# Head-pair preparation moved to the front of its slot, with the sequence mixing spaced by other products

## The chip, the cores and the metric

The kernel runs on one core of a Trainium2 chip. The metric is the device time of one execution in microseconds; a second number, the span, runs from the first to the last instruction that the profiler recorded. TensorE multiplies matrices and transposes (a product with an identity matrix), VectorE, ScalarE and GpSimd (POOL) do element-wise work, SyncE (SP) issues most of the loads and stores. ScalarE has a queue for loads of its own. Each engine runs its own instructions in the order in which they stand in its list and waits where an operand isn't there.

## The reference

Three layers, all in float32, with B = 2 sequences of S = 768 positions, 8 heads of 64, model width 512:

```
scores = q k^T / 8 - slope(head) * distance          # kept: 96 local positions and the first 8 (global)
a = softmax(scores);  x = a v                        # x: (2, 768, 512), heads side by side
u = x + (x^T U V)^T                                  # sequence mixing, U 768x32, V 32x768
x = u + relu(u w_ch1) w_ch2                          # 512 -> 2048 -> 512
xk, xr = mixes of x with x shifted by one position
out = sigmoid(xr w_r) * (relu(xk w_k)^2 w_v)         # 512 -> 1024 -> 512
```

The weights arrive as 64-bit floats and are turned into pairs of float32r numbers (high and low part) on the chip; each large product is three products of such parts.

## The kernel before

The body first runs attention in windows (`attention_windows`, lines 155 to 382), then the second layer, then the third. Work is written as lists of small steps; `weave` (line 594) merges several lists by the relative place of each step in its own list, so a list of two steps put beside one of sixteen has its steps after the fourth and the twelfth. The merged order is a priority: the framework's planner then fixes each engine's list, mostly in that order, but lets a later instruction go ahead where it thinks an earlier one isn't ready yet.

**Head pairs.** The 16 heads of both sequences make 8 pairs. For each pair, `load_qk` (line 170) loads Q and K, four loads of 192 KB on SP's queue, into one buffer for Q and one for K. `load_v` (line 182) loads V, twice, with a shifted copy, in six loads into two buffers. `qprep` (line 253) transposes Q by six TensorE instructions into two PSUM banks and copies them scaled to QS on ScalarE in two copies. `kprep` (line 266) does the same for K into KK, and GpSimd copies the first 32 columns to each block (line 282). `score(pp, i0)` (line 285) multiplies for two blocks of 128 positions and two heads; VectorE adds the mask and takes the minimum (line 301), ScalarE takes the exponential and its sum (line 304). `norm` (line 307) divides, on GpSimd (line 315). `trans` (line 321) transposes the result on TensorE, copied by VectorE or ScalarE (lines 472 and 474). `pv` (line 332) multiplies with V.

**Slots.** `slot(pp)` (line 348) lists the steps in which pair pp is scored, pair pp-1 is transposed and multiplied with V, and pair pp+1 is prepared: load of V; scores of blocks 0 and 1; transposes; `qprep` of the next pair; scores of blocks 2 and 3; normalisation; transposes; `kprep` of the next pair; loads of Q and K for the pair after the next; the rest. There are nine slots. The PSUM banks are in two groups of four: scores and first products of each layer use group "a", everything else group "t". The `in` pool has one buffer for each of Q and K, so the load of the next Q waits until the present Q is transposed.

**Side work.** Beside the slots, `side` (line 625) places other steps: constants in slot 1, `u_steps(0)` in slot 5, `st_split(0)` in slot 6, the first products of the second layer in slots 7 and 8. `CONV` spreads weight conversions (`bg`). `u_steps(b)` (line 498) is the sequence mixing of sequence b, 16 steps: six groups of transposes (`tr`), `gms` with 12 products with U, `gs` with six small copies and sums on ScalarE and VectorE in a chain, and eight products with V (`hm`, line 525), each added to `yp` by VectorE (line 530). `u_split` (line 546) splits one 512-column chunk of `yp` into high and low parts, a ScalarE copy and a VectorE subtraction (lines 551 and 552). `m_ch1` (line 567) and `m_ch2` (line 582) are the products of the second layer, 12 each. After the last slot come `u_steps(1)` woven with the first half of `st_ch2(0, 0)`, the other half woven with `st_split` of chunk 1 (lines 633 and 702), and from line 704 on a long run of products.

**The start.** Line 196 loads Q of pair 0 on SP, `limits` (line 49) loads the two numbers n_global and n_local on ScalarE's queue and turns them into floats on VectorE, `warm` runs products with zeros on TensorE, then K of pair 0 is loaded on SP. Lines 375 to 381 then prepare pair 0, with `windows` (line 214), the mask, in between, and load Q and K of pair 1 and V of pair 0.

Of the kernel before, what the change touches and what calls it, by code (L numbers as in the profile page):

```python
# [19 lines left out]
NT = S // 128  # L20
# [13 lines left out]
def body(tc, out, q, k, v, n_global, n_local, U, V, w1, w2, mu_k, mu_r, wk, wv, wr):  # L34
    nc = tc.nc
    with ExitStack() as ctx:
# [11 lines left out]

        def limits():
            nraw = const.tile([128, 2], I64, name="nraw")  # L50
            nfl = const.tile([128, 2], F32, name="nfl")
            nc.scalar.dma_start(out=nraw[:, 0:1], in_=n_global.rearrange("(o n) -> o n", o=1).partition_broadcast(128))
            nc.scalar.dma_start(out=nraw[:, 1:2], in_=n_local.rearrange("(o n) -> o n", o=1).partition_broadcast(128))
            nw = nraw.bitcast(I32).rearrange("p (n w) -> p n w", w=2)
            nlo = nraw.bitcast(U32).rearrange("p (n w) -> p n w", w=2)
            nc.vector.tensor_copy(out=nf, in_=nw[:, :, 1])
            nc.vector.tensor_copy(out=nfl, in_=nlo[:, :, 0])
            nc.vector.scalar_tensor_tensor(out=nf, in0=nf, scalar=4294967296.0, in1=nfl, op0=ALU.mult, op1=ALU.add)
# [96 lines left out]
        def attention_windows(pool, actx, cctx, bctx, bank, ecopy):  # L155
# [13 lines left out]

            def load_qk(pp, names="qk"):  # L170
                b, p = PRS[pp]
                z = st[pp]
                for nm in names:
                    src = q if nm == "q" else k
                    z[nm] = in_p.tile([128, NT, 2, D], F32, tag=nm + "in", name=nm + "in")
                    for t in range(2):
                        nc.sync.dma_start(out=z[nm][:, :, t, :],
                                          in_=src[b, 2 * p + t].rearrange("(t p) d -> p t d", p=128))
# [16 lines left out]

            load_qk(0, "q")
            limits()
            wz = ac.tile([128, 512], mybir.dt.bfloat16, name="wz")
            nc.vector.memset(wz, 0.0)
# [6 lines left out]

            warm(8)
            load_qk(0, "k")


# [3 lines left out]
            def windows():  # L214
# [12 lines left out]
                m1 = scratch(F32, 256, "m1")  # L227
                nc.vector.tensor_scalar(out=m0, in0=relf, scalar1=0.0, scalar2=None, op0=ALU.is_ge)
                nc.vector.tensor_scalar(out=m1, in0=relf, scalar1=nl, scalar2=None, op0=ALU.is_lt)
                nc.vector.tensor_tensor(out=m0, in0=m0, in1=m1, op=ALU.mult)  # L230
                nc.gpsimd.memset(DW, BIG)
                nc.vector.copy_predicated(W1[:, 0:96], m0[:, 32:128].bitcast(U32), relf[:, 32:128])
# [7 lines left out]
                nc.vector.tensor_copy(out=W0, in_=W1[:, 128:256])  # L240
                nc.vector.tensor_tensor(out=W0[:, 0:32], in0=W0[:, 0:32], in1=dg, op=ALU.min)


# [104 lines left out]
            def slot(pp):  # L348
                o = pp - 1
                cur, nxt, pre = pp < NPR, pp + 1 < NPR, pp >= 1  # L350
                s = []

                def add(cond, f, *a):
                    if cond:
                        s.append(lambda: f(*a))
                add(cur and pp, load_v, pp)
                add(cur, score, pp, 0)
                add(pre, trans, o, 0, 0)
                add(pre, trans, o, 1, 0)
                add(nxt, qprep, pp + 1)  # L360
                add(cur, score, pp, 2)
                add(cur, norm, pp, 0, 3)
                add(pre, trans, o, 0, 1)
                add(pre, trans, o, 1, 1)
                add(nxt, kprep, pp + 1)
                add(pp + 2 < NPR, load_qk, pp + 2)
                add(cur, score, pp, 4)
                add(cur, norm, pp, 3, 6)
                add(pre, trans, o, 0, 2)
                add(pre, trans, o, 1, 2)  # L370
                add(pre, pv, o, 0)
                add(pre, pv, o, 1)
                return s

            qprep(0)
            warm(3)
            windows()
            kprep(0)
            warm(3)
            load_qk(1)  # L380
            load_v(0)
            return {"zt_p": zt_p, "slot": slot, "constants": constants}

        def path(general):
            if general:
                attention_general()
            with ExitStack() as pctx:
# [110 lines left out]
                def u_steps(b):  # L498
# [38 lines left out]

                    steps += [gms, gs]
                    for c0, c1 in ((0, 512), (512, 768)) if b == 0 else ((0, 256), (256, 768)):
# [81 lines left out]
                else:  # L621
                    actx, bctx, cctx = ExitStack(), ExitStack(), ExitStack()
                    A = attention_windows(pool, actx, cctx, bctx, bank, ecopy)
                    xt_p[0] = A["zt_p"]
                    side = {1: lambda: [A["constants"]], 5: lambda: u_steps(0), 6: lambda: st_split(0, slot_a),
                            7: lambda: st_ch1(0, 0, slot_b)[:2], 8: lambda: st_ch1(0, 0, slot_b)[2:]}
# [5 lines left out]
                open_slots("sd")  # L632
                weave(u_steps(1), st_ch2(0, 0)[:2])
                actx.close()
# [64 lines left out]
                def st_mix(c, which, mk):  # L699
                    return [lambda kk=kk: m_mix(c, which, kk, mk) for kk in range(4)]  # L700

                weave(st_ch2(0, 0)[2:],
                      [lambda kk=kk: u_split(1, kk, slot_d) for kk in range(4)])
                weave(st_ch1(0, 1, slot_c), [lambda kk=kk: u_split(2, kk, slot_d) for kk in range(4)])
# [53 lines left out]
```

## Time and profile before

| what | value |
|---|---|
| runs shown | 572.84, 572.85, 568.08 us; median 572.84 |
| profiled execution | 567.52 us |
| its span | 565.7 us, 7722 instructions |
| TensorE busy (matmul) | 537.9 us, 95% of the span |
| VectorE, ScalarE, GpSimd busy | 324.4 us (57%), 230.4 us (41%), 182.9 us (32%) |
| mean granted TensorE clock | 0.985 of full speed |

Matmuls are pipelined and their ends are modelled, so a busy share of TensorE is no share of its peak. Busy times of stages, waits and the timeline are read from the same execution.

### The profile page before, as it was taken

To read this page: it belongs to the slowest core of one execution; us is meant where nothing else is said; L and a number is where in the kernel's file an instruction comes from. 1 tells how busy PE (TensorE), PEld (TensorE's weight loads), DVE (VectorE), ACT (ScalarE), POOL (GpSimd) and SP (SyncE) were. 2 spreads that over 40 slices of the span, in tenths; PEclk is the share of its full clock that TensorE was granted. 3 is DMA by queue.
4 is the path that set the end of the run, shared out by engine and by line. 5 is a ranking of instruction groups with operands and counts; after the bars stand their busy time and mean duration, and the time that the engine had idled before them with its cause. 6 is when DMAs were issued, how large, how long until landed. Compare 5 with 4: busy or idle time off the path is not lost.

```text
span 565.7 us, 7722 instructions
## 1 busy us (share of the span) xinstructions
PE 537.9 (95%) x2814; PEld 435.2 (77%) x2814; DVE 324.4 (57%) x703; ACT 230.4 (41%) x525; POOL 182.9 (32%) x223
## 2 busy tenths in 40 slices
PE   6898779899799999999999999999999999999996
PEld 3676657587588888888888888888788888888886
DVE  4657598998798726364282855579833442243101
ACT  3888678774445204032222242144361243124200
POOL 1555533770253104040120340254571244024200
PEclk9898899999899999999999999999999999999999
DMA  8865745444036402213040404004101000100011
GB/s 162 162 159 117 184 115 146 158 126 149 1 111 187 148 1 80 69 40 109 1 151 0 123 27 149 0 1 148 39 0 38 19 20 0 38 19 20 1 38 43
DMA packets 60206, 43.84 MB, mean 78 GB/s; under 512 B 51648, under 2 KB 51904, under 8 KB 60160
## 3 DMA queue, kind: packets, MB, share of 16 engines
q1 hardware_dynamic: 59872, 43.27, 27.2%
q8 instruction: 24, 0.39, 0.3%
q14 instruction: 22, 0.18, 0.1%
q10 hardware_dynamic: 288, 0.00, 0.0%
HBM read 40.11 MB, written 3.15 MB: 76 GB/s over the span
## 4 chain that ended last, share of the span: by engine, by line
PE 79%; DVE 8%; ACT 7%; POOL 2%; issue 2%; SPq 1%; DMA 1%; POOLq 0%; DVEq 0%; ACTq 0%
PE aps L575 23%; PE bps L588 20%; PE pvs L693 12%; PE kps L666 10%; PE prs L682 6%; ACT P L304 3%; PE s L294 2%; DVE cvc L423 2%; PE tp L329 2%; POOL P L315 2%; PE xb L342 1%; DVE cvc L425 1%; DVE P L301 1%; DMA qin<-in_q_dram 1%; PE hps L527 1%
## 5 line engine op out<-in xcount | busy, mean ns | idle before, releaser
L588 PE MATMUL bps<-rs,w2s 128*128 128x512 f32 x576 | 134.5, 393 | 0.5 <-DVE xt L474 0.3
L575 PE MATMUL aps<-us,w1s 128*128 128x512 f32 x576 | 133.9, 390 | 0.0
L588 PEld LDWEIGHTS bps<-rs,w2s 128*128 128x128 f32 x576 | 109.1, 190 | 23.7 <-DVE xt L474 0.5
L575 PEld LDWEIGHTS aps<-us,w1s 128*128 128x128 f32 x576 | 107.8, 188 | 22.5 <-issue 0.2
L578 ACT ACTIVATE rs<-aps 128x512 fp32r<-128x512 f32 x48 | 28.2, 593 | 102.8 <-PE aps L575 102.8
L666 PE MATMUL kps<-mix,wk 128*128 128x512 f32 x288 | 66.1, 389 | 1.2 <-DVE kf L671 1.2
L666 PEld LDWEIGHTS kps<-mix,wk 128*128 128x128 f32 x288 | 54.0, 188 | 12.8 <-DVE kf L671 1.6
L693 PE MATMUL pvs<-wv,kh 128*128 128x512 f32 (+1 forms) x208 | 61.8, 373 | 0.0
L579 DVE SCALAR_TENSOR_TENSOR rs<-aps,rs 128x512 fp32r<-128x512 f32 x48 | 32.8, 686 | 45.5 <-ACT rs L578 45.5
L315 POOL TENSOR_SCALAR P<-P,sm 128x256 f32<-128x256 f32 (+1 forms) x96 | 47.8, 518 | 28.9 <-DVE sm L311 10.6
L423 DVE SCALAR_TENSOR_TENSOR cvc<-cvc,cvt 128x512 uint32<-128x512 uint32 (+2 forms) x55 | 51.6, 940 | 9.7 <-ACT cvc L422 8.3
L422 ACT ACTIVATE cvc<-stg 128x512 f32<-128x512 f32 (+2 forms) x55 | 36.2, 665 | 44.9 <-DMA stg<-in_moe_w_ch_dram 18.2
L592 DVE TENSOR_TENSOR yp<-bps,yp 128x512 f32<-128x512 f32 (+1 forms) x64 | 33.9, 551 | 29.8 <-PE bps L588 29.8
L304 ACT ACTIVATE P<-P,nm 128x256 f32<-128x256 f32 (+1 forms) x96 | 46.2, 484 | 11.6 <-DVE nm L301 11.3
L432 POOL TENSOR_TENSOR w2s<-cvc,w2s 128x512 fp32r<-128x512 f32 x16 | 23.5, 1485 | 70.0 <-ACT w2s L430 70.0
L432 POOL TENSOR_TENSOR w1s<-cvc,w1s 128x512 fp32r<-128x512 f32 x16 | 23.6, 1492 | 69.2 <-ACT w1s L430 69.1
L648 POOL TENSOR_SCALAR mixt<-yp,mu 128x512 f32<-128x512 f32 (+1 forms) x32 | 21.6, 681 | 74.3 <-DVE mixf L650 29.8
L425 DVE SCALAR_TENSOR_TENSOR cvc<-stg,cvc 128x512 uint32<-128x512 uint32 (+1 forms) x54 | 44.8, 839 | 0.4
L693 PEld LDWEIGHTS pvs<-wv,kh 128*128 128x128 f32 x208 | 38.1, 188 | 6.9
L673 POOL TENSOR_TENSOR kl<-kf,kh 128x512 fp32r<-128x512 f32 x24 | 31.0, 1293 | 31.1 <-ACT kh L672 31.1
L301 DVE CUSTOM_DVE_ANT_0 P<-s,DW 128x256 f32<-128x256 f32 (+1 forms) x96 | 33.5, 395 | 10.8 <-PE s L294 10.7
L693 PE MATMUL pvs<-wv,kl 128*128 128x512 f32 (+1 forms) x104 | 38.8, 373 | 0.0
(104 smaller groups left out, 640.8 us busy)
## 6 DMA issues: line engine op xcount, KB each, us to landing
stg<-in_moe_w_ch_dram SPq DMA_DIRECT2D x32, 512.0 KB, 4.0
stg<-in_moe_w_k_dram SPq DMA_DIRECT2D x8, 512.0 KB, 3.7
stg<-in_moe_w_v_dram SPq DMA_DIRECT2D x8, 512.0 KB, 3.7
qin<-in_q_dram SPq DMA_DIRECT2D x16, 192.0 KB, 3.5
kin<-in_k_dram SPq DMA_DIRECT2D x16, 192.0 KB, 3.4
vin<-in_v_dram SPq DMA_DIRECT2D x16, 192.0 KB, 3.4
out_dram<-sg SPq DMA_DIRECT2D x11, 256.0 KB, 2.0
stg<-in_moe_w_r_dram SPq DMA_DIRECT2D x4, 512.0 KB, 3.8
```

Source lines behind the costliest of these rows:

```text
L301: nc.vector.tensor_tensor_reduce(out=P[:, t, 0:n], in0=sps[t][:, 256 * x:256 * x + n], in1=W, scale=2.0 ** -(2 * p + t + 1), scalar=TOP, o ...
L304: nc.scalar.activation(out=P[:, t, 0:n], in_=P[:, t, 0:n], func=ACTF.Exp, scale=-1.0, bias=z["nm"][:, i, t:t + 1], accum_out=z["sm"][:, i, ...
L315: nc.gpsimd.tensor_scalar(out=Pl, in0=Pl, scalar1=z["sm"][:, i, t:t + 1], scalar2=1.0, op0=ALU.mult, op1=ALU.mult)
L422: nc.scalar.activation(out=c.bitcast(F32), in_=Hh.bitcast(F32), func=ACTF.Copy, scale=2.0 ** -112)
L423: nc.vector.scalar_tensor_tensor(out=c, in0=c, scalar=3, in1=t, op0=ALU.logical_shift_left, op1=ALU.bitwise_or)
L425: nc.vector.scalar_tensor_tensor(out=c if plain is None else plain, in0=Hh, scalar=0x80000000, in1=c, op0=ALU.bitwise_and, op1=ALU.bitwise_or)
L432: nc.gpsimd.tensor_tensor(out=lo, in0=f, in1=hi.bitcast(F32), op=ALU.subtract)
L575: nc.tensor.matmul(ps, lhsT=wsl(("w1", g), lw, kk, f * 128, 128), rhs=us[c][:, lx, kk, :], start=(n == 0), stop=(n == 11))
L588: nc.tensor.matmul(ps, lhsT=wsl(("w2", g), lw, f, o * 128, 128), rhs=r[:, lx, f, :], start=(n == 0), stop=(n == 11))
L666: nc.tensor.matmul(ps, lhsT=wsl("wk", lw, kk, f * 128, 128), rhs=xk[:, lx, kk, :], start=(n == 0), stop=(n == 11))
L682: nc.tensor.matmul(pr, lhsT=xr[:, lx, kk, t * 128:(t + 1) * 128], rhs=wsl("wr", lw, kk, 0, 512), start=(n == 0), stop=(n == 11))
L693: nc.tensor.matmul(pv, lhsT=ks[c][lx][:, f, t * 128:(t + 1) * 128], rhs=wsl("wv", lw, f, c0, c1 - c0), start=(n == 0), stop=(n == 23))
```

## The change

In words:

- In `slot`, `qprep(pp+1)` stands ahead of the first scores of pair pp, and `kprep(pp+1)` and `load_qk(pp+2)` right behind them, ahead of the transposes of the pair before.
- Q has two buffers instead of one. K keeps one.
- K of pair 0 is loaded on ScalarE's queue, behind the two limits. The order at the start is: Q of pair 0 (SP), zeros and warm products, the part of the mask that needs no limits, the limits, K of pair 0 (ScalarE's queue), Q and K of pair 1 and V of pair 0 (SP), `qprep(0)`, the rest of the mask, `kprep(0)`. Before, the last three loads stood behind `kprep(0)`.
- Scratch for the zeros and the limits comes from the pool of the score tiles.
- Of `u_steps(0)`, the first eight steps (transposes, `gms`, `gs`) stay in slot 5 and the eight `hm` go to slot 6, ahead of the splits.
- Of the second sequence, the first eight steps of `u_steps(1)` are woven with one `m_ch2`; then three `m_ch2` follow alone, then the eight `hm`, then the splits of chunk 1 alone.

```diff
@@ load_qk
-            def load_qk(pp, names="qk"):
+            def load_qk(pp, names="qk", eng=nc.sync):
...
-                    z[nm] = in_p.tile([128, NT, 2, D], F32, tag=nm + "in", name=nm + "in")
+                    z[nm] = in_p.tile([128, NT, 2, D], F32, tag=nm + "in", name=nm + "in", bufs=2 if nm == "q" else 1)
                     for t in range(2):
-                        nc.sync.dma_start(out=z[nm][:, :, t, :],
+                        eng.dma_start(out=z[nm][:, :, t, :],
...
             load_qk(0, "q")
-            limits()
-            wz = ac.tile([128, 512], mybir.dt.bfloat16, name="wz")
+            wz = np_p.tile([128, 512], mybir.dt.bfloat16, tag="P", name="wz")
...
             warm(8)
-            load_qk(0, "k")
@@ windows: now a generator in two parts
                 nc.vector.tensor_scalar(out=m0, in0=relf, scalar1=0.0, scalar2=None, op0=ALU.is_ge)
+                nc.gpsimd.memset(DW, BIG)
+                yield
                 nc.vector.tensor_scalar(out=m1, in0=relf, scalar1=nl, scalar2=None, op0=ALU.is_lt)
                 nc.vector.tensor_tensor(out=m0, in0=m0, in1=m1, op=ALU.mult)
-                nc.gpsimd.memset(DW, BIG)
@@ slot
                 add(cur and pp, load_v, pp)
+                add(nxt, qprep, pp + 1)
                 add(cur, score, pp, 0)
+                add(nxt, kprep, pp + 1)
+                add(pp + 2 < NPR, load_qk, pp + 2)
                 add(pre, trans, o, 0, 0)
                 add(pre, trans, o, 1, 0)
-                add(nxt, qprep, pp + 1)
                 add(cur, score, pp, 2)
                 add(cur, norm, pp, 0, 3)
                 add(pre, trans, o, 0, 1)
                 add(pre, trans, o, 1, 1)
-                add(nxt, kprep, pp + 1)
-                add(pp + 2 < NPR, load_qk, pp + 2)
                 add(cur, score, pp, 4)
...
+            wins = windows()
+            next(wins)
+            limits(lambda dt, n, nm: np_p.tile([128, 2], dt, tag="P", name=nm))
+            load_qk(0, "k", nc.scalar)
+            load_qk(1)
+            load_v(0)
             qprep(0)
+            next(wins)
             warm(3)
-            windows()
             kprep(0)
             warm(3)
-            load_qk(1)
-            load_v(0)
@@ path
-                    side = {1: lambda: [A["constants"]], 5: lambda: u_steps(0), 6: lambda: st_split(0, slot_a),
+                    u0 = u_steps(0)
+                    side = {1: lambda: [A["constants"]], 5: lambda: u0[:8], 6: lambda: u0[8:] + st_split(0, slot_a),
                             7: lambda: st_ch1(0, 0, slot_b)[:2], 8: lambda: st_ch1(0, 0, slot_b)[2:]}
...
-                weave(u_steps(1), st_ch2(0, 0)[:2])
+                u1, c0 = u_steps(1), st_ch2(0, 0)
+                weave(u1[:8], c0[:1])
+                weave(c0[1:])
+                weave(u1[8:])
...
-                weave(st_ch2(0, 0)[2:],
-                      [lambda kk=kk: u_split(1, kk, slot_d) for kk in range(4)])
+                weave(st_split(1, slot_d))
                 weave(st_ch1(0, 1, slot_c), [lambda kk=kk: u_split(2, kk, slot_d) for kk in range(4)])
```

## Rows read from the trace of the kernel before

**Rows 1.** Busy times by stage: stretch and length, us busy (instructions) per engine, granted clock, DMA

```profile
0.00:9.70 9.70, 6.51 (x26) 2.84 (x27) 3.99 (x30) 3.10 (x5) 1.58 (x10) 1.00 0.75 147
9.70:19.00 9.30, 6.19 (x42) 4.05 (x41) 4.50 (x26) 7.01 (x27) 2.61 (x7) 1.00 0.94 184
19.00:31.07 12.07, 11.57 (x99) 8.99 (x98) 7.34 (x35) 9.48 (x35) 6.66 (x17) 0.86 0.67 123
31.07:41.83 10.76, 10.34 (x103) 8.11 (x102) 7.27 (x33) 9.28 (x32) 5.47 (x14) 1.00 0.83 192
41.83:55.31 13.48, 11.53 (x104) 9.42 (x103) 9.66 (x39) 11.09 (x36) 7.36 (x16) 0.87 0.62 132
55.31:69.80 14.49, 11.64 (x109) 9.78 (x107) 8.02 (x34) 10.50 (x34) 8.70 (x18) 0.88 0.70 171
69.80:87.29 17.49, 14.15 (x90) 9.88 (x89) 14.85 (x41) 13.02 (x37) 5.84 (x9) 0.90 0.41 103
87.29:101.73 14.44, 14.44 (x124) 10.70 (x123) 13.08 (x42) 12.32 (x34) 6.33 (x10) 1.00 0.64 184
101.73:133.06 31.33, 28.86 (x238) 22.32 (x237) 29.27 (x77) 21.03 (x62) 20.16 (x28) 1.00 0.46 138
133.06:157.15 24.09, 20.00 (x98) 15.18 (x96) 17.87 (x33) 11.72 (x25) 4.60 (x4) 0.93 0.16 50
157.15:565.70 408.55, 402.64 (x1798) 333.89 (x1796) 208.59 (x318) 121.82 (x207) 113.62 (x97) 1.00 0.17 56
```

**Rows 2.** TensorE's waits: who waited for whom, us, times, longest

```profile
PE hps L527 <- DVE uv L522: 6.4, 2, 3.6
...
PE tp L329 <- POOL P L315: 2.3, 5, 0.5
```

**Rows 3.** Timeline of the start: start us, us, engine, line, operation [idle before]

```profile
1.21 0.45 ACTq L53 DMA_DIRECT2D nraw<-in_n_local_dram  x1
...
1.84 1.89 SPq L177 DMA_DIRECT2D kin<-in_k_dram  x2
...
7.99 1.34 SPq L177 DMA_DIRECT2D qin<-in_q_dram  x2
...
8.28 0.85 PE L277 MATMUL kps<-ident,kin 128*128 128x128 f32 x6 [0.35 <-DMA kin<-in_k_dram]
...
13.28 0.85 PE L261 MATMUL qps<-ident,qin 128*128 128x128 f32 x6 [1.76 <-DMA qin<-in_q_dram]
...
13.95 1.05 ACT L263 ACTIVATE QS<-qps,cs 128x512 f32<-128x512 f32 x2 [1.06 <-PE qps L261]
...
16.60 2.54 POOL L315 TENSOR_SCALAR P<-P,sm 128x128 f32<-128x128 f32 x6 [6.69 <-ACT P L304]
...
16.86 0.84 ACT L280 COPY KK<-kps 128x512 f32<-128x512 f32 x2
...
19.09 0.32 POOL L282 COPY KK<-KK 128x160 f32<-128x160 f32 x1
```

**Rows 4.** TensorE's timeline in slots 3 and 4, at the K transposes

```profile
49.53 1.30 PE L277 MATMUL kps<-ident,kin 128*128 128x128 f32 x6 [1.93 <-ACT QS L263]
...
63.71 1.54 PE L277 MATMUL kps<-ident,kin 128*128 128x128 f32 x6 [2.85 <-ACT QS L263]
```

**Rows 5.** Timeline after the last slot, around the second sequence mixing

```profile
144.69 0.71 PE L527 MATMUL hps<-uv 96*128 96x256 f32 x4 [3.63 <-DVE uv L522]
145.08 1.42 DVE L530 TENSOR_TENSOR yp<-hps,yp 128x256 f32<-128x256 f32 x4 [0.54 <-PE hps L527]
...
145.56 4.54 PE L588 MATMUL bps<-rs,w2s 128*128 128x512 f32 x12 [0.16 <-DVE yp L530]
146.42 1.42 DVE L552 TENSOR_TENSOR us<-yp,us 128x256 fp32r<-128x256 f32 x4
...
150.75 2.47 DVE L530 TENSOR_TENSOR yp<-hps,yp 128x512 f32<-128x512 f32 x4
...
151.69 5.62 PE L588 MATMUL bps<-rs,w2s 128*128 128x512 f32 x24
```

More of the change, by code (lines that the diff above doesn't have):

```diff
@@ L47, in body, with limits @@
         y = yp.rearrange("p k (b s) -> p k b s", b=2)
-        def limits():
-            nraw = const.tile([128, 2], I64, name="nraw")
-            nfl = const.tile([128, 2], F32, name="nfl")
+        def limits(scratch):
+            nraw = scratch(I64, 2, "nraw")
+            nfl = scratch(F32, 2, "nfl")
             nc.scalar.dma_start(out=nraw[:, 0:1], in_=n_global.rearrange("(o n) -> o n", o=1).partition_broadcast(128))
@@ L241, in windows @@
                 nc.vector.tensor_tensor(out=W0[:, 0:32], in0=W0[:, 0:32], in1=dg, op=ALU.min)
+                yield
             KS = 160
```

## The prediction

> **What bounds the kernel now.** I read the busy times stage by stage first [rows 1], cutting where the first scores of a head pair begin: "slot p" below is the stretch in which pair p is scored while pair p-1 is transposed and multiplied with V; slots 0 to 4 are the second to sixth line, slots 5 and 6 the next two, 7 and 8 together the next. The reader should see two kernels in one. From 157.15 us on TensorE is busy 402.64 of 408.55 us at full clock: it bounds, and nothing there is touched, so it goes through the change unaltered and every microsecond won or lost before 157.15 reaches the end. Before that point no engine is full throughout. Slot 2 is the undisturbed pattern: 10.76 us, TensorE 10.34, ScalarE 9.28, both nearly full. Slots 3 and 4 hold the same attention work but last 13.48 and 14.49 us with ScalarE at 11.09 and 10.50, and TensorE's granted clock is 0.87 and 0.88 there. Slots 5 to 8 add the first sequence mixing and products, and VectorE rises to 14.85 of 17.49, 13.08 of 14.44 and 29.27 of 31.33. Second come TensorE's waits by releaser [rows 2] and third the timeline around those waits [rows 3 to 5], which say what was late.
>
> **The change part by part.** The sum is made against the profiled execution, 567.52 us (span 565.70, 1.82 around it). The three runs shown are 572.84, 572.85 and 568.08, so it lies beside the fastest and 5.3 below the median.
>
> *K of pair 0 from ScalarE's queue, limits and windows reordered.* Now SP issues Q of pair 0, then K at 1.84 us taking 1.89 [rows 3]. After, ScalarE issues K behind the two limit loads, the second of which ends at 1.66: an earlier issue by 0.2 us. ScalarE then loads its table about 1.9 us later, which nothing needs before the first QS copy; its 3.10 busy of 9.70 [rows 1] is that cover. The mask arithmetic that doesn't need the limits moves ahead of the wait for them on VectorE, which is busy 3.99 of 9.70 [rows 1]: nothing, since the scores wait for K, whose transposes start at 8.28 [rows 3], not for the mask. But with two Q buffers, SP is free to issue Q of pair 1 at 1.84, where it issued K; now it is held until 7.99 [rows 3]. So Q of pair 1 moves while K of pair 0 moves. Nothing in the trace shows two queues loading at once. Bounds: K lands 0.2 us earlier, or behind all of the new Q, 2 x 192 KB at the 184 GB/s of the next stretch [rows 1], 2.1 us later. I take 0: K and the old Q are issued first and most of Q of pair 1 follows them.
> What the row shows is one queue at work. The Trainium skill's DMA: Bandwidth & Descriptors, section "Issuing engines are not separate DMA queues", says loads from the scalar and sync queues share the same DMA engines and interleave, so that a second issuer saves only issue time. By that rule this edit wins no bandwidth, and the sum would take the late end of the bounds just given.
>
> *Slots 0 and 1.* TensorE runs its list in order. At 13.28 its Q transposes for pair 1 have waited 1.76 us for the load, with the rest of slot 0's scores queued behind them; the QS copy follows at 13.95, the KK copies at 16.86, and GpSimd's copy of the 32 shared columns only at 19.09, behind six normalisations [rows 3]. Slot 1's scores need that copy. After, Q of pair 1 has landed well before; K of pair 1 still waits for its single buffer until pair 0's K is transposed, with V of pair 0 in SP's queue beside it, so it lands about as now. All of slot 0's scores go out earlier, and kprep sits ahead of the normalisations. ScalarE must still do 12 exponentials and four copies, so I don't take the whole 1.76 plus the queueing on GpSimd (six at about 0.42 us, 2.5); I take -2.0, bounds -3.5 and 0.
>
> *Slots 2 to 4.* Same instructions, moved: 6 Q transposes with two copies, 6 K transposes with two copies and a GpSimd copy to the head of the slot, and four loads earlier on SP. In slots 3 and 4 TensorE stands 1.93 and 2.85 us before the K transposes, because the QS copies that must free a PSUM bank stand in ScalarE's list behind exponentials [rows 4]. Moved to the head, these copies fall where ScalarE waits for a first score to come through VectorE, and their transposes where banks are free. 4.78 us of waiting go. The clock of 0.87 and 0.88 says that about a quarter of these slots ran at the lower level, after such waits; a quarter of 28 us at half speed costs 3.5 us, of which half goes with the waits, 1.7. What is late next is ScalarE: its 11.09 + 10.50 = 21.6 of 27.97 us leave at most 6.4, and it will idle somewhere. I take -4.5, bounds -6.4 and -2. Slot 2: -0.3, since TensorE's 10.34 of 10.76 leaves no more than 0.4. On SP, load_qk is moved past nothing that is due sooner: V of the slot is ahead of it as now, and K waits for the K transposes with the weight loads behind it, as now.
>
> *First sequence mixing (batch 0) spread over slots 5 and 6.* The eight products of the chain's second half leave slot 5, where they waited 2.8 us for the four small copies and sums (6.4 in two times, the longer 3.6 [rows 2]), and stand among slot 6's items before the four splits. They bring eight VectorE additions into slot 6, and the splits end later. Slots 5 and 6 last 31.93 us with VectorE at 27.93, so at most 4.0 can go; the added crowd on VectorE in slot 6 can cost about as much as the additions that come into it, some 2 us beyond its idle 1.36. I take -2.0, bounds -4 and +2. Slots 7 and 8 (VectorE 29.27 of 31.33): 0.
>
> *Second sequence mixing (batch 1), after the last slot.* Now TensorE waits 3.63 us before the products of the chain and 0.16 after the first four, and the next 12 products take 4.54 at the lower clock, where 24 take 5.62 later, so 1.7 too many [rows 5]: 5.5 us in all. After, 36 products of ch2 (8.4 us at that rate) cover the chain. But they covered something: additions and splits of chunk 1. Then all eight mixing products come at the very end, about 1.6 us of products by an estimate (the four short ones take 0.71), VectorE needs 1.42 + 2.47 for their additions and 1.42 for the splits [rows 5], and the first product of the next layer waits for them. From the end of the mixing products that is 5.3 - 1.6 = 3.7 us of TensorE idle if the splits come last, less if they go between. So -5.5 + 3.7 = -1.8; I take -1.7, bounds -4 and +1 (with a slow restart).
>
> Sum: 0 - 2.0 - 0.3 - 4.5 - 2.0 - 1.7 = **-10.5 us**, 557.0 on the profiled execution's scale, 562.3 on that of the median shown. I put the time between, at 560 (zero change is then 570).
>
> **The rivals.**
> *K late.* By the bound above, 2.1 us later at the start, all else as forecast: 562. For it: DMA engines are 0.75 and 0.94 busy in the first two stretches [rows 1]. Against: K's issue is still early. The skill's rule above is this case.
> *The other engines were the bound.* TensorE's waits vanish but come back as waits for ScalarE in slots 3 and 4 and VectorE in 5 to 8; only slots 0 and 1 and the end pay: -3.5 to -4, 567. For it: VectorE at 0.93 in slots 7 and 8. Against: ScalarE's 6.4 us idle in slots 3 and 4.
> *The order written isn't the order run.* The instruction order is planned; if the planner thinks the loads late it puts Q and K preparation back behind scores: 570. For it: it already pulls scores ahead of the Q transposes in slots 3 and 4. Against: the loads get about a slot more of lead.
> *Slower: exponentials start late.* At the head of slots 0 to 6 ScalarE does the QS and KK copies, 1.05 + 0.84 us [rows 3], ahead of the exponentials; normalisation follows and the next slot's transposes wait for it. 7 x 1.89 = 13.2, the 6.8 of slots 0 to 4 not won, 3.7 won elsewhere: +9.5, 580. It decides where the copies use more than ScalarE's idle share of a slot: 10.76 - 9.28 = 1.48 in slot 2. Against: transposes now wait for GpSimd only 2.3 us in five times [rows 2], and the copies were inside the slot before too.
>
> **Chances.** Forecast 0.54, K late 0.10, other engines 0.20, order not run 0.06, slower 0.10. A measurement of this kernel can tell about 1% from no change. Forecast and K late are faster by 1.5 to 1.8%: 0.64; other engines and order not run are within 1%: 0.26; slower 0.10. Range 551 to 571: the low end is the forecast with slots 0 to 4 at their bounds and the end at -4, -16 on the profiled scale; the high end takes in the two cases within 1%; it leaves out the slower case, and about as much below.
>
> **What would show it.** Right: slots 3 and 4 near 11.5 us, no wait of K transposes for QS copies, first scores of slot 1 near 17 us, no wait at batch 1's mixing products but one of 2 to 4 us before the next layer. Wrong: K transposes of pair 0 after 9 us; slots 1 to 4 with transposes waiting for GpSimd; slots 5 to 8 longer than 63.3 us.

## The result and the profile after

The changed kernel takes 563.44 us (median of 16 runs, 561.82 to 565.40), the kernel before 568.18 (16 runs beside them); the ratio is 0.9899, interval 0.9875 to 0.9923. It is faster by 1.0%, where 1.85% (10.5 us) was forecast. Runs of one kernel differ with the granted clock (of 25 runs of the kernel before, 15 took 565.5 to 568.3 us at a mean of 0.984 to 0.991 and 10 took 570.7 to 573.3 at 0.973 to 0.979), and one run of 894.07 us, at 0.557, is left out of the first combination's figure below. The profiled execution took 562.91 us, span 561.0, against 567.52 and 565.7: 4.7 us, and these are followed here.

Busy times by stage of the kernel after, cut at the same first scores as [rows 1], with two cuts more (117.17, where slot 8 begins, and 128.87, the end of attention). Columns as in [rows 1].

```profile
0.00:9.68 9.68, 7.14 (x33) 3.62 (x33) 1.36 (x14) 3.20 (x6) 1.78 (x10) 1.00 1.03 175
9.68:17.76 8.08, 6.12 (x37) 3.96 (x36) 6.69 (x42) 6.15 (x23) 1.25 (x4) 0.87 1.18 199
17.76:28.96 11.20, 11.20 (x103) 9.01 (x102) 7.26 (x36) 10.45 (x39) 8.48 (x21) 0.94 0.66 119
28.96:39.24 10.28, 9.47 (x97) 7.47 (x96) 8.40 (x36) 9.03 (x32) 4.39 (x11) 1.00 0.98 210
39.24:49.33 10.09, 9.89 (x92) 7.56 (x91) 7.31 (x32) 8.60 (x28) 3.75 (x9) 1.00 0.73 167
49.33:62.73 13.40, 11.39 (x121) 9.29 (x119) 9.24 (x39) 12.02 (x42) 10.67 (x22) 1.00 0.74 166
62.73:73.33 10.60, 9.59 (x74) 7.35 (x73) 8.86 (x29) 8.84 (x27) 6.91 (x13) 1.00 0.93 220
73.33:89.41 16.08, 15.29 (x112) 9.32 (x111) 14.16 (x43) 13.63 (x39) 7.54 (x9) 1.00 0.52 148
89.41:117.17 27.76, 24.65 (x177) 17.96 (x176) 24.25 (x68) 18.61 (x55) 15.01 (x21) 0.94 0.34 102
117.17:128.87 11.70, 11.27 (x92) 9.04 (x91) 10.79 (x21) 5.58 (x11) 6.62 (x9) 1.00 0.43 132
128.87:150.57 21.70, 19.08 (x98) 14.23 (x96) 15.26 (x30) 8.39 (x19) 1.27 (x1) 1.00 0.16 51
150.57:561.00 410.43, 402.65 (x1796) 333.77 (x1796) 213.88 (x322) 124.87 (x213) 115.95 (x99) 1.00 0.17 56
```

Read against [rows 1]: slot 2 starts 2.1 us earlier (28.96 for 31.07) and takes 0.5 less; slots 3 and 4 take 23.49 for 27.97, 4.5 less, at full clock; slots 5 to 8 take 66.14 for 63.26, **2.9 more** (only the four together compare, since the first scores of pairs 6 and 7 are now pulled ahead in twos, between other work); the end takes 21.70 for 24.09, 2.4 less. The long run does 402.65 us of products as before (402.64), in 410.43 for 408.55: VectorE's last instruction ends 4.2 us before the end of the span before, 6.1 after. So -2.1 - 0.5 - 4.5 + 2.9 - 2.4 + 1.9 = -4.7.

TensorE's waits of the kernel after: who waited for whom, us in all, times, the longest.

```profile
PE tp L329 <- POOL P L315: 3.3, 3, 2.9
PE aps L579 <- DVE us L556: 1.9, 1, 1.9
PE s L294 <- DVE nm L301: 1.8, 2, 1.5
PE tp L329 <- ACT QS L263: 1.5, 1, 1.5
...
PE hps L531 <- DVE uv L526: 0.8, 1, 0.8
```

The 6.4 us for the mixing products of [rows 2] are 0.8, and the K transposes of [rows 4] wait no more. New are one wait each in slot 7 (2.9, for GpSimd's scaling of P), at the end (1.9, for the splits of chunk 1), at the start (1.5, for the mask) and in slot 4 (1.5, at 56.77, before transposes of P).

### The profile page after: what moved, and what is told of

Its sections match the earlier page's. It is cut to its first block, busy times and chain, and to the rows that moved or that the text cites. A ratio compares the mean times of both kernels' runs of the same rounds, so it can differ in the third digit from the quotient of the medians.

```text
span 561.0 us, 7718 instructions
## 1 busy us (share of the span) xinstructions
PE 537.7 (96%) x2814; PEld 432.6 (77%) x2814; DVE 327.5 (58%) x703; ACT 229.4 (41%) x525; POOL 183.6 (33%) x223
## 4 chain that ended last, share of the span: by engine, by line
PE 79%; DVE 7%; ACT 6%; DMA 3%; POOL 2%; issue 2%; SPq 0%; POOLq 0%; DVEq 0%; ACTq 0%
PE aps L579 22%; PE bps L592 19%; PE pvs L701 12%; PE kps L674 10%; PE prs L690 6%; PE s L294 3%; ACT P L304 3%; PE tp L329 2%; DVE cvc L427 2%; DVE cvc L429 1%; PE xb L342 1%; POOL P L315 1%; DMA stg<-in_moe_w_ch_dram 1%; PE gps L517 1%; DMA qin<-in_q_dram 1%
## 5 line engine op out<-in xcount | busy, mean ns | idle before, releaser
L579 PE MATMUL aps<-us,w1s 128*128 128x512 f32 x576 | 136.0, 393 | 1.9 <-DVE us L556 1.9
L592 PE MATMUL bps<-rs,w2s 128*128 128x512 f32 x576 | 132.8, 390 | 0.3 <-DVE xt L478 0.3
L315 POOL TENSOR_SCALAR P<-P,sm 128x256 f32<-128x256 f32 (+1 forms) x96 | 50.1, 542 | 28.8 <-DVE sm L311 14.6
L427 DVE SCALAR_TENSOR_TENSOR cvc<-cvc,cvt 128x512 uint32<-128x512 uint32 (+2 forms) x55 | 50.1, 913 | 9.6 <-ACT cvc L426 8.2
```

What stands on the lines that cost most here:

```text
L315: nc.gpsimd.tensor_scalar(out=Pl, in0=Pl, scalar1=z["sm"][:, i, t:t + 1], scalar2=1.0, op0=ALU.mult, op1=ALU.mult)
L427: nc.vector.scalar_tensor_tensor(out=c, in0=c, scalar=3, in1=t, op0=ALU.logical_shift_left, op1=ALU.bitwise_or)
L579: nc.tensor.matmul(ps, lhsT=wsl(("w1", g), lw, kk, f * 128, 128), rhs=us[c][:, lx, kk, :], start=(n == 0), stop=(n == 11))
L592: nc.tensor.matmul(ps, lhsT=wsl(("w2", g), lw, f, o * 128, 128), rhs=r[:, lx, f, :], start=(n == 0), stop=(n == 11))
```

## The experiments

Each kernel was timed beside the kernel before, but not beside the changed kernel: what is said against that one compares medians of two sets of runs. Drawing both sets anew at random many times gives, for 95%, 0.1 to 3.1 us for the 1.2 of batch 0's chain, 0.4 to 3.8 for the 1.5 of the slot's order, 0.0 to 2.7 for the 1.4 of the conversions, and nothing clear of zero for GpSimd's queue. First came four that undo one part each, to see where the 4.7 us come from; then four that repair one suspect each; then combinations. "Last copy" below is ScalarE's copy that ends a pair (L344): 28.27, 62.48 and 128.99 us for pairs 0, 3 and 7 in the kernel after, 31.18, 69.33 and 133.18 before. The start differs between executions: in the eight profiles with the start, the slot's order and the buffers of the kernel after, pair 0's last copy lies between 28.27 and 30.01 and the first scores of pair 2 between 28.96 and 30.70. The kernel after has the earliest of both.

**The limits with a buffer of their own.** In the kernel after they borrow buffers of P, and their loads are issued last.

```diff
-            limits(lambda dt, n, nm: np_p.tile([128, 2], dt, tag="P", name=nm))
+            limits(lambda dt, n, nm: st_p.tile([128, n], dt, tag="nm", name=nm))
```

> The changed kernel with the limits' scratch in another pool (the one for sums and minima), so that the two limit loads stand first on ScalarE's queue again, ahead of K of pair 0. Theory A (the late mask costs time at the start): the limits land near 5.5 us instead of 9.62, the first mask operation on scores starts near 10.7 us instead of 12.17, the 1.48 us wait of TensorE for VectorE at 12.95 goes, and the end comes 1.0 to 1.5 us earlier: 562.0 to 562.4 where the changed kernel has 563.4. Rival B (ScalarE's exponentials bound slots 0 and 1 anyway): first mask near 10.7, but slot 1 starts as now and the time stays at 563.4 within 0.4.

567.04 us, ratio to before 0.9975 (0.9942 to 1.0007): slower than the changed kernel by 3.6, against both theories. The start of this kernel, and the stretch from 1.2 to 4.8 us (columns of [rows 1]) of the kernel after and then of this one:

```profile
0.74 0.44 ACTq L52 DMA_DIRECT2D nraw<-in_n_global_dram  x1
1.75 1.05 ACTq L177 DMA_DIRECT2D kin<-in_k_dram  x2
...
8.04 1.51 PE L261 MATMUL qps<-ident,qin 128*128 128x128 f32 x6 [3.61 <-DMA qin<-in_q_dram]
```

```profile
1.20:4.80 3.60, 3.58 (x8) 1.00 (x8) 1.02 (x11) 0.00 (x0) 0.83 (x4) 1.00 0.89 185
```

```profile
1.20:4.80 3.60, 3.23 (x8) 1.03 (x8) 0.47 (x8) 1.28 (x1) 0.83 (x4) 1.00 0.28 57
```

With the limits' loads first and K right behind them, Q of pair 0, issued at 0.74 as ever, lets its transposes start at 8.04 instead of 5.93. The DMA engines moved 57 GB/s instead of 185, busy 0.28 of the time. From 7.4 to 10.7 us the granted clock was 0.50, too, so that these transposes took 1.51 us and not 0.85. So the late arrival is no sharing of bandwidth: the engines had room. The Trainium skill's DMA: Bandwidth & Descriptors, section "Issuing engines are not separate DMA queues", says that loads of all issuing engines interleave on the same DMA engines; that two queues win no bandwidth is not contradicted here, but it does not give these 2 us. What holds the loads back stays open.

**Batch 0's chain back in one slot.**

```diff
-5: lambda: u0[:8], 6: lambda: u0[8:] + st_split(0, slot_a),
+5: lambda: u0, 6: lambda: st_split(0, slot_a),
```

> The changed kernel with the sequence mixing of batch 0 back in slot 5 whole, the splits alone in slot 6. Theory A (the products moved to slot 6 push the splits against GpSimd's normalisation and the conversions in slot 7, and cost the 2.9 us wait at 103.78 and the lower clock after it): 3 to 5 us faster, 558.5 to 560.5; attention ends (last product with V) near 125 us instead of 128.9. Rival B (VectorE's sum of work bounds slots 5 to 8, whichever slot has it): 563.4 within 1. Rival C (the forecast: moving them won about 2 us): 565.4, with the wait of 2.8 us at the mixing products back.

564.61 us, ratio 0.994 (0.9905 to 0.9976), 1.2 slower than the changed kernel. Yet the last copies of pairs 3 and 7 lie 63.91 us apart, against 66.51 in the kernel after and 63.85 before: slots 5 to 8 do win back 2.6. Against that stand a start 1.2 us later (last copy of pair 0 at 29.44, with the start's code unchanged) and two places behind attention. TensorE waits 1.41 us at 130.83 for a copy of VectorE's, where the kernel after waits 0.27; and behind the wait of 1.93 for the splits, which the kernel after has too, the clock falls. The stretch two to four us into the long run (columns of [rows 1]), kernel after, then this one:

```profile
152.57:154.57 2.00, 2.00 (x10) 1.60 (x9) 2.00 (x3) 2.00 (x4) 2.00 (x2) 1.00 0.00 0
```

```profile
152.27:154.27 2.00, 2.00 (x7) 1.54 (x6) 2.00 (x3) 1.10 (x2) 2.00 (x2) 0.50 0.00 0
```

The granted clock is 0.50, the lower level (1.2 GHz), and the 92 products up to the next layer's second half take 22.62 us instead of 21.05.

**Batch 1's chain as before.**

```diff
-weave(u1[:8], c0[:1]); weave(c0[1:]); weave(u1[8:])
+weave(u_steps(1), st_ch2(0, 0)[:2])
...
-weave(st_split(1, slot_d))
+weave(st_ch2(0, 0)[2:], [... u_split(1, kk, slot_d) ...])
```

> The changed kernel with the end of attention woven as before (all of the sequence mixing of batch 1 beside two products of ch2, the other two beside the splits of chunk 1). Theory A (the chain's cover was worth 2.4 us net): 2 to 3 us slower, 565.5 to 566.4, from the end of the last product with V to the long run of products 24.1 us instead of 21.7, with a 3.6 us wait at the mixing products and the lower clock behind it. Rival B (the uncovered additions and splits cost as much as the cover won): 563.4 within 0.7.

566.10 us, ratio 0.9957 (0.9924 to 0.9991), 2.7 slower than the changed kernel; the wait of 3.6 us for the small sums is back. This part of the change is worth what the trace showed.

**The slot's order as before**, Q's second buffer, start and chains as changed.

```diff
+                add(cur, score, pp, 0)
                 add(nxt, qprep, pp + 1)
-                add(cur, score, pp, 0)
-                add(nxt, kprep, pp + 1)
-                add(pp + 2 < NPR, load_qk, pp + 2)
...  # qprep again behind the first transposes, kprep and load_qk behind the second
```

> The changed kernel with the order of steps in a slot as before, but with both Q buffers, the start and the chains as changed. Theory A (the place of the preparation in ScalarE's list is what slots 3 and 4 gained by): waits of K transposes for QS copies are back, slots 2 to 4 last 5 us longer, 568 to 569. Rival B (the early load of Q, with the second buffer, did it): K transposes don't wait over 0.5 us, and the time is 563 to 565.

564.89 us, ratio 0.9933 (0.9892 to 0.9973), 1.5 slower than the changed kernel. Pairs 0 to 3 take 35.26 us between last copies (34.21 after, 38.15 before), but pair 0's is at 31.77. The K transposes of one pair wait for a QS copy again (2.25 us at 62.56), against theory B; the time is theory B's. And slots 5 to 8 take 62.46 us there, at full clock, with the chain's move in place (66.14 after and 63.26 before, both at 0.97): the loss in the kernel after takes the new order and the move together. The row, with columns as in [rows 1]:

```profile
67.50:129.96 62.46, 58.44 (x449) 42.70 (x448) 56.95 (x157) 46.71 (x129) 32.62 (x46) 1.00 0.52 142
```

**One buffer for Q**, the order as changed.

```diff
-z[nm] = in_p.tile(..., bufs=2 if nm == "q" else 1)
+z[nm] = in_p.tile(...)
```

> The changed kernel with one buffer for Q again; the order of the slot stays as changed. Theory A (the second buffer, which lets Q of a pair load a whole slot earlier, is most of the 4.5 us that slots 3 and 4 won): the copies that end pairs 0 and 3 lie some 37 us apart instead of 34.2, TensorE waits for Q's loads by name, and the whole is 2.5 to 4 us slower than the changed kernel, 565.5 to 567. Theory B (the order of the slot alone removes the waits, because K's copy and ScalarE's Q are no longer the last thing before the next scores): 34 to 35 us between those copies, and within 1 us of the changed kernel.

566.40 us, ratio 0.9971 (0.9938 to 1.0005), 3.0 slower. The size is theory A's, the place is not: pairs 0 to 3 take 34.61, and pair 0's last copy is at 30.65, since slot 0 waits 1.59 us for Q of pair 1 at 13.77 and the first masked score comes at 13.62 (12.17 in the kernel after), behind limits' loads that go out only at 6.87. Together the two say: for slots 2 to 4 **either** part nearly suffices (38.15 to 35.26 or 34.61, both 34.21). For slots 0 and 1 they don't settle it: pair 0's last copy is late in both (31.77 and 30.65, where unchanged code gives 28.27 to 30.01), but with the old order the first scores of pair 2, at 30.41, lie within what unchanged code gives, and with one buffer the mask is late as well.

**A covering group behind batch 1's chain.**

```diff
-weave(c0[1:])
+weave(c0[1:3])
 weave(u1[8:])
+weave(c0[3:])
```

> The changed kernel with the last of the four groups of products that cover batch 1's chain put behind the chain's end instead of ahead of it. Theory A (the 1.92 us in which TensorE waits at 150.57 for the splits is a new wait of the change, and one group of 12 products, 2.72 us, behind the last sums fills it, while 24 products of 5.65 us still cover the chain up to its products): the wait falls under 0.3 us, and the whole is 1.5 to 2 us faster than the changed kernel, 561.5 to 562; in executions where the granted clock falls behind that wait, up to 3.4. Theory B (the splits on VectorE and ScalarE set the time whatever TensorE does meanwhile): the first of the long run of products starts where it did, and the time stays within 0.5.

560.73 us, ratio 0.9864 (0.9822 to 0.9906), 2.7 faster than the changed kernel. TensorE's timeline of the end, kernel after, then this one:

```profile
136.82 8.47 PE L592 MATMUL bps<-rs,w2s 128*128 128x512 f32 x36
...
150.57 21.21 PE L579 MATMUL aps<-us,w1s 128*128 128x512 f32 x92 [1.92 <-DVE us L556]
```

```profile
136.74 5.75 PE L592 MATMUL bps<-rs,w2s 128*128 128x512 f32 x24
142.32 0.52 PE L531 MATMUL hps<-uv 96*128 96x256 f32 x3
...
145.67 2.89 PE L592 MATMUL bps<-rs,w2s 128*128 128x512 f32 x12
148.39 11.95 PE L579 MATMUL aps<-us,w1s 128*128 128x512 f32 x52
```

24 products still cover the chain, the other 12 fill the wait for the splits, and it is gone.

**The limits' loads on GpSimd's queue.**

```diff
-            nc.scalar.dma_start(out=nraw[:, 0:1], ...)
+            nc.gpsimd.dma_start(out=nraw[:, 0:1], ...)   # and the same for nraw[:, 1:2]
```

> The changed kernel with the two loads of the limits issued by GpSimd's queue instead of ScalarE's. Theory A (the mask is late at the start only because the limits' loads stand behind those of Q and K of pairs 0 and 1 and land at 9.62; GpSimd's queue is free): the first masked score near 10.7 instead of 12.17, the wait of 1.48 us for it at 12.95 gone, 1 to 1.5 us faster than the changed kernel. Theory B (the loads compete for the same DMA engines and land as late, or GpSimd's issue is slow): first masked score at 12 or later, same time or up to 1 us slower.

564.19 us, ratio 0.9921 (0.9892 to 0.995): no gain. The mask is done at 10.60 (12.00 in the kernel after), as theory A had it, but its first use is at 12.49. TensorE's start in this kernel:

```profile
6.19 1.51 PE L261 MATMUL qps<-ident,qin 128*128 128x128 f32 x6 [1.40 <-DMA qin<-in_q_dram]
...
11.54 2.91 PE L294 MATMUL s<-KK,QS 64*128 64x128 f32 x20
```

Q came 0.26 us later than in the kernel after, and these transposes took 1.51 and 1.48 us where there they took 0.85 and 0.82, so the scores start at 11.54 instead of 9.68. That isn't the edit's doing: the covering group's profile, whose start is that of the kernel after, has Q at 6.07, transposes of 1.51 and 1.44 us and the first scores at 11.33. Against that profile the early mask moves pair 0's last copy by 0.1 us (28.59 for 28.73).

**Slot 6's conversions in slot 3.**

```diff
-CONV = {2: 3, 4: 2, 5: 2, 6: 2, 7: 2}
+CONV = {2: 3, 3: 2, 4: 2, 5: 2, 7: 2}
```

> The changed kernel with the two weight conversions of slot 6 done in slot 3 instead. Theory A (the 2.9 us lost in slots 5 to 8 come from batch 0's splits meeting the conversions on VectorE and GpSimd in slots 6 and 7: GpSimd's scaling of P took 0.84 us for each instead of about 0.45 there, and TensorE waited 2.91 us for it at 103.78): that wait falls under 1 us, pair 3's to pair 7's last copy 64 to 65 us instead of 66.5, some 2 us faster than the changed kernel, less what slot 3 loses to the two conversions (0 to 1 us). Theory B (the loss is that the sums of batch 0 come a slot later, whatever else runs): 66 us or more between those copies, within 0.5 us of the changed kernel, or slower by what slot 3 loses.

562.02 us, ratio 0.9883 (0.9841 to 0.9925), 1.4 faster than the changed kernel. Pair 3's last copy comes later (68.72), pair 7's at 126.71: from pair 0 on 98.02 us against 100.72 in the kernel after. The wait of 2.9 for GpSimd is gone from slot 7; one of 4.3 stands in slot 4 instead. And of 2.7 us won before the end of attention, 2.0 go behind it: a wait of 2.27 at 130.83, 0.27 in the kernel after. The rest of the profile's gain is the stretch behind VectorE's last instruction, 4.4 us for 6.1, which nothing here explains. VectorE and TensorE of this kernel there:

```profile
129.75 0.43 DVE L425 TENSOR_SCALAR cvt<-stg 128x512 uint32<-128x512 uint32 x1 [1.13 <-DMA stg<-in_moe_w_ch_dram]
130.09 1.28 DVE L478 COPY xt<-xtp 128x512 f32<-128x512 f32 x2
```

```profile
126.59 1.97 PE L508 MATMUL xtp<-ident,yp 128*128 128x128 f32 x16
130.83 3.04 PE L592 MATMUL bps<-rs,w2s 128*128 128x512 f32 x12 [2.27 <-DVE xt L478]
```

VectorE's next instruction in line is a conversion whose weights have not landed; the copies of finished transposes stand behind it.

**The repairs together.** The covering group and the early conversions (first expectation); with them, batch 1's six copies on ScalarE (second, diff below); and the covering group and those copies with batch 0's chain in one slot, conversions unmoved (third).

```diff
-                        ecopy(out=z[i], in_=ps)
+                        (ecopy if b == 0 else nc.scalar.copy)(out=z[i], in_=ps)
```

> The two gains together on the changed kernel: one group of covering products behind batch 1's chain, and slot 6's two conversions in slot 3. Theory A (the two are independent, 2.7 us and 1.4 us below the changed kernel): about 559.3. Theory B (both are cut by the same thing: what is won before the batch 1 chain is given back in the wait for its copies, 2.27 us at 130.83 with the conversions early, because VectorE's queue stands behind a conversion that waits for its load): 560 to 561, with that wait of 2 us or more still there.

> The version with the covering group behind the chain and slot 6's conversions in slot 3, and the six copies of batch 1's transposes all on ScalarE instead of two in three on VectorE. Theory A (the 2.27 us before the first covering products are VectorE's queue standing behind a conversion whose load has not landed; ScalarE is idle 5.78 us right there): that wait falls under 0.8 us and the whole is 1 to 2 us faster than without this edit. Theory B (ScalarE's own casts of batch 0 to 1, 1.33 us, and six copies of 0.59 us in line take the wait's place): wait unchanged or 1 us longer, same time or slower.

> The covering group behind batch 1's chain, batch 0's chain as before the change (its eight products in slot 5, its splits alone in slot 6), and batch 1's six copies on ScalarE; the conversions where the changed kernel has them. Theory A (slots 5 to 8 lose 2.6 us by the chain's move, and undoing it gave nothing in the time only because VectorE's queue was blocked at batch 1's copies, 1.41 us, and the clock fell behind the wait at 150.27): 2 to 3 us faster than the covering group alone, some 558 to 559. Theory B (moving the chain is neutral, and what the trace showed was one execution's): within 0.5 us of the covering group alone, 560.2 to 561.2.

558.89, 557.70 and 558.01 us; ratios 0.9821 (0.9767 to 0.9875), 0.9798 (0.975 to 0.9846) and 0.9812 (0.9761 to 0.9863). The first adds its two gains as theory A had it, though the wait of theory B is there (2.35 us). In the second that wait is gone; the same two lines of TensorE:

```profile
127.81 1.97 PE L508 MATMUL xtp<-ident,yp 128*128 128x128 f32 x16
129.54 3.00 PE L592 MATMUL bps<-rs,w2s 128*128 128x512 f32 x12
```

The third, with batch 0's chain in one slot and the copies on ScalarE, is 2.7 us below the covering group alone (0.4 to 4.5 by the same drawing). How much of that is the chain's and how much the copies' was not tried.

**The start once more**, on the second of these: limits on GpSimd's queue, and in slot 0 the first scores ahead of pair 1's Q.

```diff
+                if pp: add(nxt, qprep, pp + 1)
                 add(cur, score, pp, 0)
+                if not pp: add(nxt, qprep, pp + 1)
```

> The version with the covering group, the early conversions and batch 1's copies on ScalarE, and at the start the limits' loads on GpSimd's queue with pair 0's scores ahead of pair 1's Q in slot 0. Theory A (both starting points of pair 0 have to move at once: with the limits early, the first masked score waits for the first scores, which stand 0.75 us behind pair 1's Q): first masked score before 11.5, the wait of 1.4 us for the mask at 12.94 gone, pair 0's last copy near 28 instead of 29.0, 0.7 to 1.4 us faster, 556.3 to 557. Theory B (the start is set by when Q and K of pair 0 land, and what they lose to the limits' loads in the race costs what the mask gains): within 0.5 us, 557.2 to 558.2.

558.22 us, ratio 0.9832 (0.9791 to 0.9873): 0.5 slower, which the runs can't tell from nothing. First masked score at 12.03, the wait for the mask gone, pair 0's last copy at 29.37, where the version without this edit has 29.01; Q is 0.2 us later (6.20 for 6.00) and its transposes take 1.51 us, as in the covering group's profile. The time is theory B's; that the loads' race sets the start isn't shown. The best version is the second of the repairs, 2% below the kernel before.

## Why the prediction was right, and by half

Direction and range held, but the range says little: it runs from 551 to 571, with no change at 570. Step by step:

- **Slots 0 and 1, forecast -2.0: -2.1.** Right in this execution, with luck: in the eight profiles with the same start the gain against the one profile of the kernel before runs from 0.4 to 2.1, and this one has the largest. Which part of the change makes it stays open.
- **Slots 2 to 4, forecast -0.3 and -4.5: -0.5 and -4.5.** Right: the waits of [rows 4] are gone, the clock is at 1.00 where it was 0.87 and 0.88. What was not seen is that the earlier load alone, or the order alone, does most of it.
- **Batch 1's chain, forecast -1.7: -2.4,** and -2.7 by undoing it. The new wait before the next layer, 2 to 4 us in the forecast, is 1.92. It was treated as the price of covering the chain; the covering group showed that 24 products suffice for that, and the price need not be paid.
- **Slots 5 to 8, forecast -2.0, bounds -4 and +2: +2.9.** This is the step that failed: "the added crowd on VectorE in slot 6 can cost about as much as the additions that come into it" and "Slots 7 and 8: 0". Of the miss of 5.8 us in all, it is 4.9. What was forecast to go did go: the wait for the chain's small sums, 2.8 us before, is 0.8. Two things came in its place. The first is a new wait. The crowd does not stay in slot 6: all four splits now run in slot 7, three of them beside the second half of GpSimd's scaling of pair 6's P. (Before, two ran beside the first half, and no wait for P was over 0.5 us.) GpSimd, then VectorE, then TensorE of the kernel after, in stretches so short that the view doesn't merge like instructions:

```profile
98.76 0.48 POOL L315 TENSOR_SCALAR P<-P,sm 128x256 f32<-128x256 f32 x1 [3.37 <-DVE sm L311]
99.20 1.70 POOL L436 TENSOR_TENSOR w2s<-cvc,w2s 128x512 fp32r<-128x512 f32 x1
100.89 1.43 POOL L315 TENSOR_SCALAR P<-P,sm 128x256 f32<-128x256 f32 x1
102.30 1.42 POOL L315 TENSOR_SCALAR P<-P,sm 128x256 f32<-128x256 f32 x1
103.70 0.47 POOL L315 TENSOR_SCALAR P<-P,sm 128x256 f32<-128x256 f32 x1
```

```profile
96.77 0.69 DVE L556 TENSOR_TENSOR us<-yp,us 128x512 fp32r<-128x512 f32 x1
...
99.70 1.75 DVE L556 TENSOR_TENSOR us<-yp,us 128x512 fp32r<-128x512 f32 x1
101.38 0.68 DVE L429 SCALAR_TENSOR_TENSOR cvc<-stg,cvc 128x512 uint32<-128x512 uint32 x1
101.98 0.88 DVE L556 TENSOR_TENSOR us<-yp,us 128x512 fp32r<-128x512 f32 x1
102.78 0.68 DVE L556 TENSOR_TENSOR us<-yp,us 128x512 fp32r<-128x512 f32 x1
```

```profile
103.78 0.33 PE L329 MATMUL tp<-ident,P 128*128 128x128 f32 x1 [2.91 <-POOL P L315]
```

One scaling is done in 0.48 us, the median of all 96. Then GpSimd's own conversion stands in line, 1.70 us where it takes 1.28 alone, and the split beside it takes 1.75 where one takes 0.69 alone: it ends 0.55 us behind the conversion. The next two scalings take 1.43 and 1.42 us, and each ends 0.26 us behind a pair of VectorE instructions with two inputs in SBUF (at 102.06 and 103.46). The three after them, with no such instruction beside them, take 0.47 or 0.48 again; TensorE had waited for the second of the long ones. (The 0.84 us in the expectation for the conversions is the mean of these five.) The Trainium skill's SBUF — State Buffer, section "Who interferes with whom", says that a VectorE instruction with two inputs in SBUF contends with a GpSimd instruction that reads SBUF, and that the ports they share are an exclusive lock. The trace agrees: in each of these meetings one instruction ends a fraction of a microsecond behind the other engine's. The forecast used VectorE's busy share alone and no wait for GpSimd in these slots, though rival "exponentials start late" named that very wait ([rows 2], 2.3 us in five times).

The second is not a wait. TensorE's idle time in slots 5 to 8 is not longer than before; its busy time is, for the same number of instructions at the same granted clock. Slots 5 to 8 (columns of [rows 1]) of the kernel before, the kernel after, and that with batch 0's chain back in one slot:

```profile
69.80:133.06 63.26, 57.45 (x449) 42.90 (x449) 57.20 (x158) 46.37 (x129) 32.34 (x46) 0.97 0.48 139
```

```profile
62.73:128.87 66.14, 60.80 (x449) 43.67 (x449) 58.06 (x157) 46.66 (x129) 36.08 (x51) 0.97 0.50 138
```

```profile
63.92:127.46 63.54, 57.97 (x450) 42.45 (x449) 56.42 (x158) 47.24 (x129) 36.78 (x51) 0.97 0.54 144
```

Idle are 5.81, 5.34 and 5.57 us. TensorE's timeline of these stretches, which puts like products in a row on one line, has 93, 123 and 94 lines: the products come in more and shorter pieces. So the new wait only took the old one's place, and the 2.9 us stand in the 3.35 us of busy time. Whether a short piece costs by itself, or the engine stands in it in a way that the modelled ends count as busy, stays open. That the chain's move brings the loss is shown by taking it back (2.6 us between the last copies of pairs 3 and 7), and that it takes the new slot order too by the old order (62.46). Moving the conversions removes this wait as well, and from pair 0's last copy to pair 7's saves 2.7 us, but a wait of 4.3 us comes in slot 4, so it can't say which meeting cost what. The clock has a part in it too: in the profile of the limits' buffer, the same wait of 2.91 was not followed by a lower clock, and slots 5 to 8 took 64.62 us.
- **The start, forecast 0.** K was early, as forecast (transposes at 7.26 for 8.28). "Nothing, since the scores wait for K ... not for the mask" was wrong: the limits' loads went behind those of Q and K, at 4.11 and 5.81, the first masked score moved from 10.69 to 12.17, and TensorE waited 1.48. Two edits that brought the mask back won nothing clear of noise. Why is open: in their profiles the first transposes took 1.51 us, as in two profiles whose start is that of the kernel after. "Nothing in the trace shows two queues loading at once" overlooked the limits' own loads, on ScalarE's queue beside Q's in the kernel before.
- **The dense part, "unaltered".** Right for its products; the 1.9 us after VectorE's last instruction were not foreseen. That stretch is 4.2 to 4.4 us in the profiles of seven of the fourteen kernels and 5.9 to 6.6 in the other seven; two kernels that differ only in where two conversions run stand on either side. What sets it stays open.

Of the rivals, "K late" showed in the first experiment, at 3.6 us, though with idle DMA engines and not by the bandwidth that it was priced by. "The other engines were the bound" put the gain at 3.5 to 4 us, nearer to the 4.7 than the forecast's 10.5, but not where it arose: slots 3 and 4 won what the forecast said.

## What to carry to other kernels

Work moved out of a crowded slot lands beside other work: before costing the move by the busy share of one engine, list what VectorE and GpSimd run at the same moment in the slot that receives it, with the durations that their instructions have when they overlap. A gain ahead of a serial chain reaches the end only if the chain's own copies are not queued behind an instruction that waits for a load; look at the first idle time behind the gain, in the same trace. And cover a chain with just as much work as it lasts: what is left over covers the wait at its end.

## What the runs showed of the hardware that was not expected

- The wait of 1.92 or 1.93 us before the long run stands in the profiles of seven kernels (the kernel after and those of the limits' buffer, chain 0, the slot's order, one Q, GpSimd's queue and the early conversions). In four the granted clock stayed at 1.00, in three it was 0.50 two to four us later, which cost 1.6 us; in the five profiles with the covering group, which lack that wait, it stayed at 1.00. The changed kernel's 16 runs have a mean granted clock of 0.987 to 0.996. That the waits removed are the reason was not tried.
- TensorE's first transposes of a run take 0.85 us in some executions and 1.51 in others, with the same code. In the profile of the limits' buffer the granted clock was 0.50, the lower level (1.2 GHz), while they took 1.51 (row below, columns of [rows 1]). In the profile of GpSimd's queue the column shows 1.00 with 1.51 as well, but its record of the clock begins only at 10.22 us, about when the products become fast, and what lies ahead of the record is counted as 1.00. In the five profiles with 1.51 and 1.00 the record begins at 9.66 to 10.60 us, in the eight with 0.85 at 4.18 to 5.47. A 1.00 at the very start of a run is no evidence of the higher level.

```profile
7.40:10.70 3.30, 2.67 (x9) 1.58 (x9) 2.52 (x14) 1.05 (x2) 0.00 (x0) 0.50 1.24 198
```
- Where two loads of the limits were issued first on ScalarE's queue, all loads went with 57 GB/s in the next 3.6 us (90 in the kernel before); where they were issued behind the others, or on GpSimd's queue, with 179 to 185.
